# Row factors of a layer norm moved from the rows to the products, part of another norm moved to GpSimd, and a new order of all engines

## The chip, the cores and the metric

One core of a Trainium2 chip runs the whole program, and the metric is the time of one execution in device microseconds. Most executions of a kernel agree within 0.3%, so times are medians of several runs. A ratio is the mean time of one kernel's fast runs over that of the other's fast runs of the same rounds, with a 95% interval. It is therefore not quite the ratio of the medians quoted beside it. A profile is one more execution of the same program. Its span is about 1.7 us shorter than the reported time.

## The reference, cut to what matters

```python
def _layernorm(x, axis=-1, eps=1e-5): ...
xn = _layernorm(x)                              # x: 2048 x 640, the first layer norm
# branch A: attention, 32 heads of 20 channels
p = _softmax(q @ k.T * Dh ** -0.5)              # 32 x 2048 x 2048 exponentials
s = (p @ v) @ wo
# branch B
h = _gelu(_layernorm(xn) @ w1)                  # the second layer norm
hs = shifted_by_1_and_2_rows(h) @ w2
x1 = xn + hs
g = _silu(x1 + _gelu(_layernorm(x1) @ w3) @ w4)
out = x + s * g
```

The second layer norm acts on rows whose mean is already zero. All that is left of it is one factor for each row. Such a factor commutes with the product by w1.

## The kernel before

The program is a list of tasks. A planner in the kernel's own source books a duration for each of them, and a latency for each transfer. From these it makes one fixed order of instructions for every engine before anything runs.

```python
self.dma_bw = 280.0                              # bytes per ns
t.lat = self.dma_lat0 + nbytes / self.dma_bw     # dma_lat0 = 1900 ns, booked for every transfer
C_SP = 660                                       # ns of queue time booked for one transfer
# ... first layer norm, one task for each 128 rows ...
T("dve", c_dve(D, "4x"), lambda e, ...: e.tensor_scalar(dst_of(n), xn[:, n, :], mv[:, li, 0:1], rs[:, li:li + 1],
                                              op0=ALU.subtract, op1=ALU.mult), ...)
# ... and, for the rows whose statistics ScalarE made:
T("act", c_act(D) + 40, lambda e, ...: e.activation(xn[:, n, :], xn[:, n, :], AF.Identity, bias=sv[:, 7, ...], scale=sv[:, 6, ...]), ...)
# ... second layer norm and w1, for each chunk of 512 rows ...
T("dve", c_dve(KC * 516, "1x"), fy, ...)         # y2c = xnT * row factors, all of a chunk in one multiply
for m in range(KC):
    h, wa = self.mm_tile(f"w1_{ch}_{m}", ...)    # products of y2c and w1
    T("dve", c_dve(512), lambda e, ...: e.tensor_copy(hx[:, ch, m, :], self.wbank(h)[:, 0:512]), ...)
# ... softmax normalisation of one group of heads and one chunk of queries ...
T("dve", ..., lambda e: e.tensor_copy(Ob, PV bank), ...)
T("sp", ...: dz <- sums)   T("sp", ...: ZT <- dz)                  # spread the sums over the partitions
T("dve", c_dve(16, "recip"), lambda e: e.reciprocal(RZ, ZT), ...)
T("sp", ...: dr <- RZ)     T("sp", ...: RB <- dr, broadcast, 256 KB)   # store and load again
T("dve", c_dve(512, "1x"), lambda e: e.tensor_tensor(dst, Ob, RB, op=ALU.mult), ...)
```

(The cuts are marked by dots, and the last lines are shortened to what moves where.) Two engines share the exponentials. ScalarE takes most of them with its exponential function, and VectorE the rest through integer arithmetic. A table of blocks says how many go to VectorE.

## Time and profile before

| | before |
|---|---|
| time, median of 4 runs | 891.04 us (890.24 to 892.52) |
| span of the profiled run | 889.4 us |
| first exponential starts | 36.26 us |
| last exponential ends | 878.10 us |
| ScalarE idle in between | 16.2 us |

ScalarE is the bound, as the prediction shows. So the execution is cut in three at its first and its last exponential. The view of stretches below gives the length of each, then the busy time and instruction count of TensorE, its weight loads, VectorE, ScalarE and GpSimd, and last the granted TensorE clock (the share of full speed that TensorE was allowed), and the DMA's share and rate.

```profile
0.00:36.26 36.26, 23.83 (x670) 14.79 (x670) 27.24 (x92) 25.33 (x48) 23.77 (x47) 1.00 0.46 143
36.26:878.10 841.84, 802.08 (x14914) 348.30 (x14912) 689.27 (x896) 825.66 (x853) 14.07 (x22) 1.00 0.21 58
878.10:889.40 11.30, 3.34 (x56) 0.99 (x48) 7.84 (x14) 0.00 (x1) 0.00 (x0) 0.70 0.21 73
```

Three groups of VectorE's instructions in that kernel (busy us, mean ns of one, then the idle time just before them and what ended it):

```profile
L1479 DVE TENSOR_TENSOR arena<-arena 128x512 bf16<-128x512 f32 x28 | 19.3, 689 | 16.1 <-DMA arena<-recips 15.8
...
L1695 DVE CAST arena<-psum 128x512 bf16<-128x512 f32 x20 | 13.7, 687 | 2.3 <-PE psum L771 2.1
...
L1682 DVE TENSOR_TENSOR arena<-arena 128x2580 bf16<-128x2580 bf16 x2 | 5.7, 2838 | 0.0
```

The last two are the evictions of w1's products (each copies a product out of PSUM, the memory that TensorE writes) and half of the row scaling that the change removes. The first is the multiply by the broadcast reciprocals.

### The profile page before, as it was taken

The page shows a single profiled execution, that of the slowest core. Times are in us where ns is not written, and L with a number is a line of the kernel's source. Part 1 is how long each engine was busy: PE and PEld are TensorE (multiplying, and loading weights), DVE is VectorE, ACT ScalarE, POOL GpSimd, SP SyncE. Part 2 cuts the span into 40 slices and gives each one's busy share as a digit, 9 for nine tenths or more (in the row PEclk, how much of TensorE's full clock was granted, in tenths as well). Part 3 has the DMA queues.
Part 4 walks back from the last instruction along what each step waited for, and adds up shares of the span by engine and source line. Part 5 has one row for each costly group of instructions (what it writes and reads, how often), then busy time and mean ns, then how long its engine had stood idle before and what let it go on. Part 6 is the DMA issues. An engine that isn't in the chain of part 4 may idle for free.

```text
span 889.4 us, 34152 instructions
## 1 busy us (share of the span) xinstructions
PE 829.2 (93%) x15630; PEld 364.1 (41%) x15630; DVE 724.4 (81%) x1000; ACT 851.0 (96%) x900; POOL 37.8 (4%) x69
## 2 busy tenths in 40 slices
PE   4999999999999999999998999999999799998996
PEld 2434333334444433344443544433434344444453
DVE  7756888887888899989776779987878679797895
ACT  6899999999999999999998999999999999999994
POOL 7310000000000000000000000000000000010000
PEclk9999999999999999999999999999999999999998
DMA  6003300012210013222223031222222201114322
GB/s 222 11 14 87 94 22 25 25 43 77 80 48 29 22 46 86 62 61 57 62 53 98 20 95 35 72 84 59 54 60 51 82 10 53 47 53 126 105 63 76
DMA packets 83548, 54.81 MB, mean 62 GB/s; under 512 B 52556, under 2 KB 77340, under 8 KB 83276
## 3 DMA queue, kind: packets, MB, share of 16 engines
q1 hardware_dynamic: 83404, 52.62, 21.1%
q8 instruction: 123, 2.02, 0.9%
q14 instruction: 21, 0.17, 0.1%
HBM read 37.91 MB, written 10.63 MB: 55 GB/s over the span
## 4 chain that ended last, share of the span: by engine, by line
ACT 45%; PE 27%; DVE 19%; DMA 8%; issue 1%; SPq 0%
ACT arena L1404 42%; PE psum L771 11%; PE psum L1380 8%; DVE arena L1345 4%; DVE arena L1431 4%; DMA arena<-recips 4%; PE psum L1362 3%; PE psum L1319 3%; PE psum L1354 2%; DMA recips<-arena 2%; DVE arena L970 2%; DMA queries<-arena 1%; ACT arena L1756 1%; ACT arena L1698 1%; DVE arena L1682 1%
## 5 line engine op out<-in xcount | busy, mean ns | idle before, releaser
L1404 ACT ACTIVATE arena<-psum 128x1024 bf16<-128x1024 f32 x836 | 779.9, 1036 | 16.5 <-PE psum L1362 5.6
L1380 PE MATMUL psum<-arena 128*32 128x512 bf16 x4992 | 380.0, 381 | 11.5 <-ACT arena L1404 9.5
L771 PE MATMUL psum<-arena 128*32 128x320 bf16 (+1 forms) x5952 | 360.3, 335 | 7.8 <-DVE arena L1161 3.5
L1431 DVE TENSOR_SCALAR arena<-psum 128x1024 uint16<-128x1024 f32 x188 | 229.1, 1218 | 52.9 <-PE psum L1362 51.8
L1345 DVE TENSOR_SCALAR arena<-arena 128x4096 uint16<-128x4096 uint16 (+1 forms) x236 | 230.1, 1008 | 5.4 <-PE psum L1354 4.1
L771 PEld LDWEIGHTS psum<-arena 128*32 128x32 bf16 x5952 | 147.9, 97 | 148.0 <-issue 27.4
L1380 PEld LDWEIGHTS psum<-arena 128*32 128x32 bf16 x4992 | 106.8, 95 | 145.6 <-ACT arena L1404 102.6
L1319 PE MATMUL psum<-arena 128*22 128x512 bf16 x1672 | 161.6, 381 | 2.0 <-DVE arena L1466 1.7
L1354 PE MATMUL psum<-arena 128*22 128x512 bf16 x1504 | 123.3, 380 | 2.1 <-DVE arena L1345 1.9
L1362 PE MATMUL psum<-arena 32*128 32x512 bf16 x800 | 83.7, 386 | 14.3 <-ACT arena L1404 6.6
L1319 PEld LDWEIGHTS psum<-arena 128*22 128x22 bf16 x1672 | 42.4, 92 | 54.2 <-issue 7.5
L1362 PEld LDWEIGHTS psum<-arena 32*128 32x128 bf16 x800 | 21.4, 91 | 98.8 <-ACT arena L1404 81.7
L1354 PEld LDWEIGHTS psum<-arena 128*22 128x22 bf16 x1504 | 36.4, 92 | 45.5 <-DVE arena L1345 10.6
L1753 DVE CAST arena<-psum 128x512 bf16<-128x512 f32 x48 | 33.0, 687 | 14.1 <-PE psum L771 14.1
L1205 DVE CAST arena<-psum 128x512 bf16<-128x512 f32 x40 | 27.3, 685 | 18.1 <-PE psum L771 18.1
L1479 DVE TENSOR_TENSOR arena<-arena 128x512 bf16<-128x512 f32 x28 | 19.3, 689 | 16.1 <-DMA arena<-recips 15.8
L1550 DVE SCALAR_TENSOR_TENSOR arena<-psum,arena 128x320 bf16<-128x320 f32 x32 | 15.5, 487 | 15.4 <-PE psum L771 15.4
L970 DVE BATCH_NORM_STATS2 arena<-arena 128x6 f32<-128x320 bf16 x52 | 23.0, 482 | 2.8 <-DMA arena<-in_A_x_dram 2.8
L1466 DVE COPY arena<-psum 128x512 f32<-128x512 f32 x28 | 19.2, 687 | 3.6 <-PE psum L1354 2.8
L1767 DVE TENSOR_TENSOR arena<-psum,arena 128x320 bf16<-128x320 f32 x32 | 15.5, 485 | 6.8 <-PE psum L771 6.8
L1756 ACT ACTIVATE arena<-arena 128x12288 bf16<-128x12288 bf16 x2 | 20.9, 10444 | 0.0
L1069 PE MATMUL psum<-arena 128*32 128x128 bf16 x320 | 9.3, 246 | 12.2 <-DVE arena L984 11.8
(101 smaller groups left out, 281.2 us busy)
## 6 DMA issues: line engine op xcount, KB each, us to landing
arena<-in_B_w_dram SPq DMA_DIRECT2D x48, 160.0 KB, 2.6
arena<-recips SPq DMA_DIRECT2D x28, 256.0 KB
arena<-arena SPq DMA_DIRECT2D x124, 32.0 KB, 1.9
arena<-in_B_w_dram SPq DMA_DIRECT2D x4, 960.0 KB, 5.3
arena<-in_A_x_dram SPq DMA_DIRECT2D x8, 320.0 KB, 6.1
arena<-in_A_x_dram SPq DMA_DIRECT2D x16, 160.0 KB, 2.5
out_dram<-arena SPq DMA_DIRECT2D x16, 160.0 KB, 1.8
arena<-keys SPq DMA_DIRECT2D x28, 80.0 KB
```

The lines of the kernel that those rows point to most:

```text
L771: ins = e.matmul(pb[32 * c:32 * c + 32, 0:N], lhsT(k, c), rhs(k, c), start=(k == 0), stop=(stop and k == nk - 1), tile_position=(0, 32 * c))
L970: lambda e, li=li, n=n, hh=hh: e.bn_stats(st[:, li, 6 * hh:6 * hh + 6], xn[:, n, hD * hh:hD * hh + hD]),
L1205: T("dve", c_dve(512), lambda e, h=h, c=c: e.tensor_copy(KS[:, 512 * c:512 * c + 512], self.wbank(h)[:, 0:512]), reads=[wa], writes=[A("KS ...
L1319: ins = e.matmul(pb[32 * i:32 * i + 22, 0:512], VA[:, ql, kts[i // 2], i, :], PT[:, slots[i // 2][0].slot, 512 * (i % 2):512 * (i % 2) + 512],
L1345: T("dve", c_dve(w, "4x"), lambda e, v=v, dst=dst: e.tensor_scalar(dst, U[:, ub, 0:w], 0.5, EXP_B[v], op0=ALU.mult, op1=ALU.add), reads=ha ...
L1354: ins = e.matmul(pb[32 * i:32 * i + 22, 0:512], wv, dst[:, at:at + 512].bitcast(BF16), start=first, stop=final, tile_position=(0, 32 * i))
L1362: return e.matmul(out, self.KT[32 * i:32 * i + 32, b, 128 * kt:128 * kt + 128], self.QT[32 * i:32 * i + 32, b, 512 * qc:512 * qc + 512], s ...
L1380: ins = e.matmul(out[32 * c:32 * c + 32, :], self.KT[:, b, 128 * kt + 32 * c:128 * kt + 32 * c + 32], self.QM[:, gb, 2 * a + jj, :], start ...
L1404: lambda e: e.activation(self.PT[:, hp.slot, :], self.psum[:, 512 * hs.slot:512 * hs.slot + 1024], AF.Exp, scale=cfg.scale),
L1431: ins = e.tensor_scalar(U[:, ub, 1024 * at + 512 * k:1024 * at + 512 * k + w], self.psum[:, 512 * hd.slots[k]:512 * hd.slots[k] + w], a_ex ...
L1753: T("dve", c_dve(512), lambda e, h=h, fc=fc, i=i: e.tensor_copy(GT[:, i, fc, :], self.wbank(h)[:, 0:512]), reads=[wa], writes=at, name=f"g ...
L1756: T("act", 2750 + c_act(2 * FC * 512), lambda e: e.activation(GT[:, :, :, :], GT[:, :, :, :], AF.Gelu_apprx_tanh), reads=gta, writes=gta, ...
```

## The change

It has three parts, which the diff shows cut to its core: the row factors move into the evictions of w1's products, four of the sixteen first-norm tiles go to GpSimd, and the planner books transfers differently, with new due times, a new table of blocks and a few more planner settings that are not shown.

```diff
-        self.dma_bw = 280.0
+        self.dma_bw = 223.0
-            t.lat = self.dma_lat0 + nbytes / self.dma_bw
+            t.lat = self.dma_lat0 + nbytes / self.dma_bw + dlat      # dlat: -840 for the reciprocals' store, +1100 for their load ...
-C_SP = 660
+C_SP = 400
-        self.DUE = dict(k0=-37.9, k1=-9.1, ...)
+        self.DUE = dict(k0=100.3, k1=-164.3, ...)                    # all due times
-        self.ND = ([2, 2, 3, 3], ... [4, 2, 3, 2])                   # blocks of exponentials for VectorE: 94
+        self.ND = ([1, 2, 3, 3], ... [4, 3, 1, 2])                   # 95
+        self.POOLN = [1, 9, 13, 15]
...
-            T("dve", c_dve(D, "4x"),
+            pool = ve_out and n in cfg.POOLN
+            T("pool" if pool else "dve", 160 + 0.86 * D if pool else c_dve(D, "4x"),      # subtract, then multiply
...
+            if n in self.cfg.POOLN:
+                T("pool", 160 + 0.86 * D, ... op0=ALU.mult, op1=ALU.add) ...               # instead of ScalarE
...
-            T("dve", c_dve(KC * 516, "1x"), fy, ...)
             for m in range(KC):
+                T("sp", C_SP * len(ranges), fr, ...)                 # row factors of this tile, broadcast, 256 KB
...
-                T("dve", c_dve(512), ... e.tensor_copy(hx[:, ch, m, :], self.wbank(h)[:, 0:512]), ...)
+                T("dve", c_dve(512), ... e.tensor_tensor(hx[:, ch, m, :], self.wbank(h)[:, 0:512], RR[:, r, :], op=ALU.mult), ...)
```

## The prediction

> **What bounds the kernel now.** I read the page of the profile first: busy time by engine, then the 40 slices, then the chain that ended last.
>
> ```profile
> PE 829.2 (93%) x15630; PEld 364.1 (41%) x15630; DVE 724.4 (81%) x1000; ACT 851.0 (96%) x900; POOL 37.8 (4%) x69
> ...
> PE   4999999999999999999998999999999799998996
> PEld 2434333334444433344443544433434344444453
> DVE  7756888887888899989776779987878679797895
> ACT  6899999999999999999998999999999999999994
> ...
> ACT 45%; PE 27%; DVE 19%; DMA 8%; issue 1%; SPq 0%
> ```
>
> ScalarE (ACT) is the bound: 96% busy, a 9 in nearly every slice, and the largest share of the chain. Its idle time is 889.4 - 851.0 = 38.4 us. TensorE is a close second, so it decides whether ACT has something to read. The table of groups says what ACT does and for whom it waits:
>
> ```profile
> L1404 ACT ACTIVATE arena<-psum 128x1024 bf16<-128x1024 f32 x836 | 779.9, 1036 | 16.5 <-PE psum L1362 5.6
> ```
>
> That is 836 exponentials at 779.9/836 = 0.933 us each in a row (the 1036 ns of one overlap). The timeline of ACT alone shows where the 38.4 us lie:
>
> ```profile
> 36.26 75.28 ACT L1404 ACTIVATE arena<-psum 128x1024 bf16<-128x1024 f32 x81 [0.48 <-PE psum L1362]
> 112.32 30.85 ACT L1404 ACTIVATE arena<-psum 128x1024 bf16<-128x1024 f32 x33 [0.79 <-PE psum L1380]
> 143.75 1.02 ACT L1404 ACTIVATE arena<-psum 128x1024 bf16<-128x1024 f32 x1 [0.58 <-PE psum L1362]
> ...
> 656.31 1.02 ACT L1404 ACTIVATE arena<-psum 128x1024 bf16<-128x1024 f32 x1 [1.31 <-PE psum L1362]
> ```
>
> The first exponential starts at 36.3 us and the last ends at 878.1. Before it lies the head (layer norm, transposes, first projections) with 10.9 us of ACT idle; after it an 11.3 us tail; between them, 841.8 us of which ACT is busy 825.7 by the view of stretches, so 16.2 us idle, in about two dozen gaps of 0.2 to 1.6 us. So nothing but the count of ACT's work, the head, the tail and those gaps can move the time.
>
> What feeds the gaps is in the chain of waits in order of time (start, length, what):
>
> ```profile
> 125.69 0.60 DVE arena L1695
> 126.29 2.75 DVE arena L1682
> 129.04 1.14 DVE arena L1345
> 130.18 1.13 DVE arena L1431
> 131.32 0.17 DVE arena L1473
> 131.49 0.02 issue
> 131.50 3.08 DMA recips<-arena
> 134.59 5.06 DMA arena<-recips
> ```
>
> The 2.75 us is the old row scaling, one multiply of all of a 512-token chunk. The short reciprocal L1473 of the softmax sums stands behind it, then two transfers of 8.1 us, and this ends in ACT's gaps at 143 (0.58 and 0.17). The same picture stands at 175.9, ending at 193. Other gaps follow the same pair of transfers without a row scaling before it: 345 (0.82), 373 (0.44), 476 to 481 (2.5 in four gaps), 586 (0.44), 656 (1.5). Together 0.75 + 0.73 + 0.82 + 0.44 + 2.5 + 0.44 + 1.5 = 7.2 us of the 16.2 come out of this transfer chain.
>
> **What the Trainium skill says.** "VectorE: DVE Perf Modes", section "The perf-mode tier table": a tensor_tensor reading PSUM or fp32 runs at 1x, and so does a copy of fp32 from PSUM. The trace agrees, in two groups of the same size, one a multiply or add with a second operand and one a plain cast:
>
> ```profile
> L1767 DVE TENSOR_TENSOR arena<-psum,arena 128x320 bf16<-128x320 f32 x32 | 15.5, 485 | 6.8 <-PE psum L771 6.8
> ...
> L1266 DVE CAST arena<-psum 128x320 bf16<-128x320 f32 x32 | 15.4, 488 | 5.2 <-PE psum L771 4.3 <-PE psum L1069 0.7
> ```
>
> 485 against 488 ns: a multiply inside an eviction is free. "GPSIMD Engine Reference", section "Engine selection": one-input elementwise work is roughly line-rate there, two-input work some 2x slower. The trace has a one-input TENSOR_SCALAR on 128x176 in 340 ns where nothing disturbs it. "TensorEngine Tiling (Array Packing)", section "Key Properties": changing the tiling mode drains TensorE. The trace agrees: at 484.4 eight matmuls of 320 columns are followed by scores of the other shape after 0.38 us where eight such take 0.27 otherwise, some 0.1 us per change.
>
> **The change, part by part.**
>
> *Row factors.* Removed: four multiplies of 2826 to 2839 ns on VectorE, 11.3 us. Added: nothing in count, since the 20 casts of w1's products (687 ns) become multiplies by a row-factor tile; by the comparison above, still 687. The products use the unscaled transposed rows, whose factors commute with the matmul. The price is transfers: one 1 MB broadcast (5.1 us from issue to landing) becomes 20 of 256 KB in 32 issues, 5 MB. At the 1 MB in 5.1 us of the trace, about 200 GB/s, an estimate, that is 26 us of transfer, in the stretch between 90 and 240 us or so where the DMA share is 5 to 32%. Seven buffers run ahead. I take it as hidden. VectorE is not the bound, so its 11.3 us are worth only what they bring forward: the reciprocals at 131 and 181.
>
> *First layer norm.* Rows 1 and 9 leave VectorE (about 0.39 us each) and rows 13 and 15 leave ACT: 5.1 us for six, 0.85 each, so ACT loses 1.7 us in the head. On GpSimd one such of 640 elements is an estimate from the 340 ns for 176: 0.8 to 1.2 us. Rows 13 to 15 were three in series on ACT from 26.5 to 29.0, and the last transposes (30.15) waited for them; now one on ACT runs beside two on GpSimd. In the built order 140 instead of 220 matmuls of 320 columns stand ahead of the first scores. After the last transposes the old order has 88 + 4 matmuls of 512 columns (at 47 ns) and 28 of 320 (34 ns), 5.3 us; the new one 60 + 4 and 40, 4.4 us. I book 2.0 us for the head: 1.2 from the norms, 0.8 from the matmuls, a little under the 0.9 that they differ by.
>
> *Split of the exponentials.* The table of blocks goes from 94 to 95 and each moves two tiles from ACT to VectorE: 834 exponentials, -2 x 0.933 = -1.9 us of ACT. VectorE gets 188 tiles in one piece and two in halves: four halves of some 0.69, +2.8 us. Its wide steps change from 140 long and 96 short to 156 and 68: 16 x 1.196 - 28 x 0.652 = +0.9. VectorE in sum: -11.3 + 2.8 + 0.9 - 0.8 = -8.4 us. TensorE: 64 fewer column-shaped score matmuls (0.43 us per eight) is -3.5; 16 more row-shaped in four groups, 4 x 0.33 = +1.3; 12 more of the value products, +0.6; six more changes of shape there and back, 216 visits for 210, +1.2. In sum -0.4: nothing. TensorE stays as near to the bound as it was.
>
> *Order.* All engines are reordered. The old planner put the broadcast of reciprocals at 1900 ns + 256 KB at 280 GB/s = 2.8 us, where the trace has 5.06; the new one books 1900 + 1175 + 1100 = 4.2. It also books 400 instead of 660 ns of queue time per issue. So the steps that wait on this chain should be placed where their data has arrived. This, with the earlier reciprocals, is where the 7.2 us of gaps can come back. A new order makes new gaps of its own; I book 6.5 us net out of the 16.2. The tail is built as before: four transposes and multiplies after the last value product, then the four last output tiles; its last value products have 8 fewer fillers of 34 ns ahead, -0.3.
>
> Sum: -1.9 - 2.0 - 6.5 - 0.3 = -10.7 us of span, 889.4 to 878.7; the reported time was 1.7 above the span, so 880.4.
>
> **Rivals.** (a) The 20 broadcasts sit in the one in-order queue of SyncE and delay the reciprocal chain. The waits of that queue show 27.6 us in front of the second transfer already; in the new order up to eleven row-factor issues stand between the sums' first transfer and its second. For it: each such broadcast must wait for its buffer. Against it: a normalisation round has some 26 us and the chain needs about 11. Were it so, gaps of 1 to 2 us would come back in four or five rounds, and the time would be 884 to 888. (b) TensorE becomes the bound: its 93% hide shape changes and the clock (0.92 in the slices around 467 and 689). Then removing VectorE's and ACT's work gives nothing but the head: 886. Against it: between 36 and 878 us it is busy 802.1 of 841.8 us, so 39.7 idle against ACT's 16.2. (c) GpSimd's norms are slow or delay the row factors' powers behind them on that in-order engine: the head then gains nothing, 882. (d) The order is near perfect: all 16.2 us of gaps go instead of 6.5, 871.
>
> **Range and chances.** The certain part is 1.9 of ACT; the head is between 0 and 4, the gaps between +2 and -13. That makes 872.5 to 888 the range for 8 in 10. Faster by over 2% needs 873.3, all of the gaps and the head: 0.09. Slower by over 2% needs 18 us of new waits in an order planned with better numbers: 0.03.
>
> **What would show it.** ACT at 834 exponentials and about 847.5 us busy (-1.9, -1.7); VectorE near 716; w1's evictions as multiplies at about 687 ns; first exponential near 34.3; ACT idle between first and last exponential near 10 instead of 16.2; the tail near 11. I am wrong if the w1 multiplies are slower or wait for the row factors, if ACT's gaps lie behind the transfer of reciprocals as before, or if the gaps now come from TensorE with VectorE and DMA long done.

## The result, and the profile after

| | before | after | difference |
|---|---|---|---|
| time, median of 4 runs | 891.04 | 885.78 (884.17 to 886.2) | -5.3 |
| ratio | | 0.9936 [0.9918, 0.9954] | |
| span of the profiled run | 889.4 | 884.1 | -5.3 |
| head, to the first exponential | 36.26 | 35.65 | -0.6 |
| middle, ScalarE busy | 825.66 | 823.33 | -2.3 |
| middle, ScalarE idle | 16.2 | 14.1 | -2.1 |
| tail, after the last exponential | 11.30 | 11.04 | -0.3 |

The change is 0.6% faster, which is the "same" of the prediction, and the time lies inside the range, 5.4 us above the 880.4 of the prediction's sum. The differences sum to the 5.3 us. They come from the view of stretches after:

```profile
0.00:35.65 35.65, 20.01 (x592) 12.83 (x596) 28.07 (x86) 23.61 (x46) 30.37 (x50) 1.00 0.46 145
35.65:873.06 837.41, 800.30 (x14962) 348.22 (x14957) 680.52 (x889) 823.33 (x851) 12.55 (x24) 1.00 0.24 63
873.06:884.10 11.04, 2.53 (x52) 0.80 (x44) 7.61 (x13) 0.00 (x0) 0.00 (x0) 0.78 0.22 76
```

In the head, TensorE and ScalarE work less than before, yet the stretch is hardly shorter. GpSimd is the engine that grew, from 23.77 to 30.37 us. VectorE grew by 0.8 us although two norms had left it.

The page of the changed kernel, with the busy times, the chain that ended last and the exponentials' group:

```profile
PE 822.8 (93%) x15594; PEld 361.9 (41%) x15594; DVE 716.2 (81%) x986; ACT 846.9 (96%) x896; POOL 42.9 (5%) x74
...
ACT 55%; PE 19%; DVE 17%; DMA 5%; POOL 1%; issue 1%; POOLq 0%
...
L1444 ACT ACTIVATE arena<-psum 128x1024 bf16<-128x1024 f32 x834 | 777.8, 1038 | 14.4 <-PE psum L1420 5.0
```

ScalarE's share of the chain rose from 45% to 55%, and that of the DMA fell from 8% to 5%. That is the direction the change meant. Its groups that answer to those shown of before, and the two kinds of norm on GpSimd:

```profile
L1519 DVE TENSOR_TENSOR arena<-arena 128x512 bf16<-128x512 f32 x28 | 19.2, 686 | 11.5 <-DMA arena<-recips 11.4
...
L1734 DVE TENSOR_TENSOR arena<-psum,arena 128x512 bf16<-128x512 f32 x20 | 13.7, 687 | 8.7 <-PE psum L782 8.7
...
L999 POOL TENSOR_SCALAR arena<-arena 128x640 bf16<-128x640 bf16 x2 | 5.1, 2534 | 0.1
...
L1037 POOL TENSOR_SCALAR arena<-arena 128x640 bf16<-128x640 bf16 x2 | 1.7, 875 | 1.8 <-DVE arena L1032 1.8
```

The multiply in the eviction takes 687 ns as the cast did, so the row scaling is indeed free. The wait for the reciprocals fell from 15.8 to 11.4 us, but did not go. On GpSimd a norm written as multiply-then-add takes 875 ns, and one written as subtract-then-multiply 2534 ns.

The largest cluster of gaps in the changed kernel stands at 209 us. The chain of waits (start, length, what) leads to it:

```profile
197.41 0.17 DVE arena L1513
197.58 0.02 issue
197.60 4.04 DMA recips<-arena
201.64 0.02 issue
201.66 5.53 DMA arena<-recips
207.19 0.02 issue
207.21 0.04 DVE arena L1519
207.25 0.57 issue
207.82 1.23 DVE arena L1471
```

The pair of transfers took 9.6 us. VectorE stood 2.86 us before its multiply, TensorE 2.43 us behind VectorE, and ScalarE 2.18 us behind TensorE, as the three timelines show:

```profile
207.21 0.69 DVE L1519 TENSOR_TENSOR arena<-arena 128x512 bf16<-128x512 f32 x1 [2.86 <-DMA arena<-recips]
...
209.18 0.40 PE L1388 MATMUL psum<-arena 32*128 32x512 bf16 x4 [2.43 <-DVE arena L1471]
...
209.62 1.02 ACT L1444 ACTIVATE arena<-psum 128x1024 bf16<-128x1024 f32 x1 [2.18 <-PE psum L1388]
```

Then TensorE's matmuls ran slowly for 4 us. The first of the next two lines is eight score matmuls in that stretch, the second the same eight a little later:

```profile
210.16 1.01 PE L1420 MATMUL psum<-arena 128*32 128x512 bf16 x8
...
214.66 0.60 PE L1420 MATMUL psum<-arena 128*32 128x512 bf16 x8
```

The granted clock from 208 to 216 was 0.78 and 0.80 in windows of 4 us, and 1.00 on both sides. ScalarE's gaps of the whole cluster, 2.18 + 0.57 + 0.68 and five smaller ones of 0.17 to 0.28, sum to 4.5 us of the 14.1.

The planner's own bookings tell where the chip left the plan. It had booked the first exponential at 31.5 us, and it came at 35.65. The exponential at 138 us ran 4.3 us behind its booking, and the one at 245 us 8.9 behind. From there to the end the distance stayed between 8.4 and 10.7. So most of what the plan missed was lost in the head and around 209. The plan of the kernel before, read the same way, was 3.5 us short at the first exponential and 12.4 at the end of the last. The two plans end the last exponential at 865.7 and 863.6 us. By the planner's own numbers, each with its own bookings, the change thus promised 2.1 us there, and the chip gave 5.0. The 10.7 us of the prediction stood in neither plan.

### The profile page after: what moved, and what is told of

The parts are those of the page before. It is cut to its first block, busy times and chain, and to the rows that moved or that the text cites. A ratio compares the mean times of both kernels' runs of the same rounds, so it can differ in the third digit from the quotient of the medians.

```text
span 884.1 us, 34138 instructions
## 1 busy us (share of the span) xinstructions
PE 822.8 (93%) x15594; PEld 361.9 (41%) x15594; DVE 716.2 (81%) x986; ACT 846.9 (96%) x896; POOL 42.9 (5%) x74
## 4 chain that ended last, share of the span: by engine, by line
ACT 55%; PE 19%; DVE 17%; DMA 5%; POOL 1%; issue 1%; POOLq 0%
ACT arena L1444 53%; PE psum L782 8%; PE psum L1420 6%; DVE arena L1371 5%; DVE arena L1471 4%; DMA arena<-recips 3%; PE psum L1345 2%; PE psum L1388 2%; DMA recips<-arena 2%; PE psum L1380 1%; ACT arena L1809 1%; DVE arena L984 1%; ACT arena L1825 1%; DVE arena L1805 1%; DVE arena L1225 1%
## 5 line engine op out<-in xcount | busy, mean ns | idle before, releaser
L1420 PE MATMUL psum<-arena 128*32 128x512 bf16 x4928 | 375.7, 381 | 8.0 <-ACT arena L1444 6.6
L1471 DVE TENSOR_SCALAR arena<-psum 128x1024 uint16<-128x1024 f32 (+1 forms) x192 | 231.5, 1206 | 42.1 <-PE psum L1388 41.3
L1345 PE MATMUL psum<-arena 128*22 128x512 bf16 x1668 | 161.8, 381 | 1.2 <-DVE arena L1506 0.6
L1380 PE MATMUL psum<-arena 128*22 128x512 bf16 x1520 | 126.5, 380 | 2.5 <-DVE arena L1371 2.2
L1519 DVE TENSOR_TENSOR arena<-arena 128x512 bf16<-128x512 f32 x28 | 19.2, 686 | 11.5 <-DMA arena<-recips 11.4
L1286 DVE CAST arena<-psum 128x320 bf16<-128x320 f32 x32 | 15.4, 488 | 10.9 <-PE psum L782 10.5
L1089 PE MATMUL psum<-arena 128*32 128x128 bf16 x320 | 8.9, 248 | 13.7 <-DVE arena L999 13.1
```

The lines of the kernel that those rows point to most:

```text
L1345: ins = e.matmul(pb[32 * i:32 * i + 22, 0:512], VA[:, ql, kts[x // 2], i, :], PT[:, slots[x // 2][0].slot, 512 * (x % 2):512 * (x % 2) + 512],
L1380: ins = e.matmul(pb[32 * i:32 * i + 22, 0:512], wv, dst[:, at:at + 512].bitcast(BF16), start=first, stop=final, tile_position=(0, 32 * i))
L1420: ins = e.matmul(out[32 * c:32 * c + 32, :], self.KT[:, b, 128 * kt + 32 * c:128 * kt + 32 * c + 32], self.QM[:, gb, 2 * a + jj, :], start ...
L1471: ins = e.tensor_scalar(U[:, ub, 1024 * at + 512 * k:1024 * at + 512 * k + w], self.psum[:, 512 * hd.slots[k]:512 * hd.slots[k] + w], a_ex ...
```

## The experiments

Theory at the outset: the gain is smaller than predicted because of two places, the head, where GpSimd holds up others, and the gaps, where the order still stands on bookings that do not hold. The rivals: the row factors' broadcasts delay the reciprocals (rival a of the prediction), GpSimd's norms are slow (rival c), or TensorE's clock takes back what is won (part of rival b). Seven kernels are meant to tell them apart. All were run beside the kernel before.

| run | time, median | ratio to before |
|---|---|---|
| e1_memset_later | 886.36 | 0.9928 [0.991, 0.9945] |
| e2_rr_small | 886.52 | 0.9932 [0.9909, 0.9954] |
| e3_norm_form | 886.12 | 0.993 [0.9902, 0.9957] |
| e4_before_rows | 893.16 | 1.0011 [0.9983, 1.0039] |
| e5_after_nopool | 886.58 | 0.9939 [0.9912, 0.9966] |
| e6_busy | 885.5 | 0.9923 [0.9899, 0.9947] |
| e7_measured | 880.81 | 0.989 [0.9868, 0.9911] |

### e1_memset_later: a clear on GpSimd moved by 1 us

In the head of the changed kernel, a VectorE instruction on four elements per partition took 2.15 us. TensorE's next four matmuls, ScalarE's next step and the first exponential waited for it. VectorE's timeline, then GpSimd's:

```profile
31.72 2.15 DVE L1166 TENSOR_SCALAR arena<-arena 128x4 bf16<-128x4 f32 x1
```

```profile
31.69 2.15 POOL L951 MEMSET arena<- 128x2048 bf16 x1
```

The two cover each other to within 0.03 us at the start. The experiment keeps everything and lets the clear wait for the small instruction:

```diff
-        T("pool", 1500, lambda e: e.memset(self.QT[:, 1, :], 0.0), writes=[A("QT0")], name="qt0")
+        T("pool", 1500, lambda e: e.memset(self.QT[:, 1, :], 0.0), reads=[A("Mq")], writes=[A("QT0")], name="qt0")
```

> The changed kernel, same order on every engine; only the clearing of one 2048-wide buffer on GpSimd now waits until the tiny VectorE scaling L1166 (128x4) has been done. Theory A (the head lost its gain because that VectorE instruction cannot start while GpSimd clears the buffer: 2155 ns instead of 237): the scaling takes some 0.24 us, the first exponential comes 1.5 to 1.9 us earlier (33.8 to 34.1 instead of 35.65), and the time falls by as much, to about 884. Rival (the scaling is slow for another reason, or the head is bound by the transposes): it still takes 2 us, or the first exponential moves less than 0.4 us; time 885.8.

Measured: the small instruction took 0.29 us, and TensorE's wait for it went.

```profile
32.57 0.29 DVE L1166 TENSOR_SCALAR arena<-arena 128x4 bf16<-128x4 f32 x1
```

In all three kernels where the clear lies over it (after, e2, e3) the instruction took 2.13 to 2.16 us. In the ten other profiled runs it took 0.24 to 0.38. That is shown. What it is worth in time is not resolved: the ratio is 0.9928 against 0.9936. The first exponential came at 34.63 us in this run, and in two repeats below at 33.79 and 34.94, so one execution's head moves by over 1 us by itself (the first load of x landed between 3.62 and 4.10 us in the traces). Here the first exponential came 1.0 us earlier and not the 1.5 to 1.9 expected. The small instruction started 0.85 us later than in the kernel after, and before it 20 matmuls at 18.70 us had taken 1.55 us in place of 1.04. And the profiled run gave its lead back at 497 us, in a gap of 4.26 us where the kernel after has 0.71. The lines of TensorE there, in the kernel after and in this one:

```profile
490.61 0.74 PE L1053 MATMUL psum<-arena 128*32 128x128 bf16 x32 [1.91 <-DVE arena L1063]
492.50 4.64 PE L782 MATMUL psum<-arena 128*32 128x512 bf16 x84 [1.16 <-DVE arena L1181]
```

```profile
486.45 0.74 PE L1053 MATMUL psum<-arena 128*32 128x128 bf16 x32 [1.91 <-DVE arena L1063]
488.98 7.57 PE L782 MATMUL psum<-arena 128*32 128x512 bf16 x84 [1.79 <-DVE arena L999]
```

It is the same order of the same instructions, but the 84 products take 7.57 instead of 4.64 us, at a granted clock of 0.52 and 0.63 in the two windows from 488 to 496. The edit alone does not decide it: e2 does not have it and ran them in 4.65, while e3 does not have it either, ran at 0.61 and 0.54 there and took 7.53:

```profile
491.29 4.65 PE L782 MATMUL psum<-arena 128*32 128x512 bf16 x84 [1.47 <-DVE arena L1519]
```

```profile
489.82 7.53 PE L782 MATMUL psum<-arena 128*32 128x512 bf16 x84 [1.61 <-DVE arena L999]
```

It need not be mere chance either. Of the looks at this order without other work for TensorE, four had their first exponential before 35 us (e1, e3, and e8 and e10 below). In all four TensorE waited 1.51 to 1.79 us just before the 84 products, and these were slow. In the three whose first exponential came at 35.65 or later (after, e2, e5) it waited 1.00 to 1.47 us and they were fast. So a shorter head may itself lengthen this wait and lose its lead here. Seven looks suggest that and do not show it.

### e2_rr_small: the row factors' broadcasts made small

```diff
+                w = 512 if KC * ch + m < 7 else 16
-   ... e.dma_start(RR[f0:f1, r, :], ... [1, 512])
+   ... e.dma_start(RR[f0:f1, r, 0:w], ... [1, w])
```

The result is wrong, since only 16 columns of most tiles are fresh, although its error stayed under the threshold of the comparison.

> The changed kernel, same order; the row-factor loads after the first seven move 16 columns instead of 512 (wrong result on purpose). Theory B (the cluster of gaps of ACT between 209 and 224 us, 4.5 us, comes from a row-factor load issued 1.3 us ahead of the reciprocals' transfer on the same queue): the transfer of reciprocals at 197.6 lands in about 2.3 instead of 4.04 us, VectorE's wait for the reciprocals' broadcast (2.86 us) shrinks to about 1, and the cluster to 1 to 2.5 us; time 883 to 884. Rival (the order itself puts the multiply by the reciprocals too early, whatever the loads do): the cluster stays above 4 us and the time at 885.8.

Measured: at 199 us the store of the reciprocals took 2.74 us from its issue to the next instead of 4.04, VectorE's wait before the multiply fell from 2.86 to 1.20, and all such waits from 11.4 to 9.9 us. ScalarE's gaps of the cluster at 209 fell from 4.5 to 1.5 us, the first of them from 2.18 to 0.52. So the local part came out nearly as expected, and the broadcasts do lengthen this chain, as rival (a) says. But the time did not move (0.9932; 883 to 884 us were expected). ScalarE's idle time in the whole middle stretch was 13.7 us against 14.1, so other gaps grew instead. Of the 1.5 us by which VectorE's waits fell, 1.1 stand before 250 us, where the broadcasts run.

### e3_norm_form: the cheap form of the norm for rows 1 and 9

```diff
-   op0=ALU.subtract, op1=ALU.mult
+   op0=ALU.mult if pool else ALU.subtract, op1=ALU.add if pool else ALU.mult
```

The result is wrong: the operands stay the mean and the factor.

> The changed kernel, same order; the two GpSimd normalisations of rows 1 and 9 do multiply-then-add instead of subtract-then-multiply (wrong result on purpose). Theory C (the 2.53 us of each is the form of the operation: the other two, multiply-then-add on the same size, took 0.875): 0.85 to 0.9 us each. Rival (it is contention with VectorE at that moment): still above 2 us. For the time: if GpSimd at 9 to 12 us is on the head's path the first exponential comes up to 1 us earlier; if the 2.2 us wait at L1166 sets the head, less than 0.3.

```profile
L999 POOL TENSOR_SCALAR arena<-arena 128x640 bf16<-128x640 bf16 x2 | 1.8, 875 | 0.1
```

The two norms took 875 ns instead of 2534. The operations alone make this difference, since operands, shapes and types are the same. TensorE's second group of transposes started at 13.87 us, against 14.60 in the kernel after. The first exponential came at 34.70, though the 2.14 us of the clear was still there. The time is 0.993. So rival (c) is right about the mechanism, at 0.7 us of the head, and too small for the times to show.

### e4_before_rows: the old order with the row factors alone

```diff
-    Gen(nc, aps, cfg).build()
+    ref = Gen(*scratch(aps), Cfg(..., old=True, rows=False, pool=False))     # the kernel before, only planned
+    ref.build(plan_only=True)
+    cfg = Cfg(..., old=True, rows=True, pool=False)
+    cfg.KEEP = ref.pl             # TensorE, ScalarE and VectorE keep the order of before
+    Gen(nc, aps, cfg).build()
```

> The kernel before with its own order kept on TensorE, ScalarE and VectorE; only the row factors are moved to w1's products (four multiplies of 2.83 us gone, 20 casts become multiplies, 1 MB load becomes 32 loads of 5 MB together). Theory D (the row factors alone are worth at most the gaps that follow the old scaling, 1.5 us): 889 to 891. Rival 1 (worth nothing, or less than nothing because of the loads): 891 to 894. Rival 2 (they carry the whole gain of the change): 886 to 887.

Measured: 1.0011. Taking 11.3 us from VectorE is worth nothing that the times resolve by itself, as the first rival of this run expected. In the profile VectorE's waits for the reciprocals rose from 15.8 us in 12 places to 20.9 in 17:

```profile
L1595 DVE TENSOR_TENSOR arena<-arena 128x512 bf16<-128x512 f32 x28 | 19.3, 689 | 21.1 <-DMA arena<-recips 20.9
```

One of them, of 3.40 us at 109.6, was followed by a wait of 2.35 for TensorE behind VectorE and a gap of 2.67 for ScalarE behind TensorE, with a granted clock of 0.82 and 0.76 in the 8 us after it. The kernel before waited 0.94 us at that place. So rival (a) happens in the old order. But the broadcasts are issued between 91 and 170 us, and up to 250 us the waits rose only from 4.8 to 6.3. The other 3.6 us of the rise stand later, where no broadcast runs, and stay unexplained. One reservation: the edit keeps the order of TensorE, ScalarE and VectorE, but the queue of transfers and GpSimd were planned again. The queue differs in 17 places, all before 200 us of the plan.

### e5_after_nopool: the new order without GpSimd's norms

The edit is as in e4, with the kernel after as the one whose order is kept, the row factors in and the norms back on VectorE and ScalarE.

> The changed kernel's order on every engine, but the four first-norm tiles 1, 9, 13 and 15 go back to where they were (two to VectorE at about 0.4 us each, two to ScalarE at about 0.9 us each); the row factors stay. Theory: the GpSimd part is worth next to nothing, because two of its four norms run as subtract-then-multiply at 2.53 us and hold TensorE's first transposes as long as they help; then 885 to 887 us (ratio to before 0.992 to 0.996) with the first exponential between 35.2 and 36.5 us. Rival: the GpSimd part carried most of the gain, then 888 to 891 us (ratio 0.997 to 1.0) with the first exponential after 37 us. With the run in which row factors alone gave 1.001 this leaves the order as the rest.

Measured: 0.9939, against 0.9936 for the whole change. The time is that of the theory, but the first exponential came at 37.49, where only the rival had expected it (after 37). That is 1.8 us later than after. As in e4, the transfers were planned again, against what the expectation says: the second and the third load of x changed places, and VectorE waited 0.77 us for the one that now came later. The middle was 0.95 us shorter. So the 1.8 us are not GpSimd's norms alone. If the 0.77 are taken off, the norms buy some 1 us of the head, an estimate, and nothing that the times resolve. The difference between e5 and e4, 0.9939 against 1.0011, is 0.7% or some 6 us: it is the new order with its block table and bookings, and these two intervals do not overlap. It is all of the gain that the times resolve. The new order without the row factors was not run, so whether it needs them is open.

### e6_busy: TensorE kept busy where its clock fell

Based on e1, TensorE multiplies the identity by itself into a bank that nobody reads, while it waits before the 84 products, and before 80 others that had taken 4.51 us in the kernel after and 6.18 in e1. The edit, shortened here, also moves one group of transposes behind two groups of value products.

```diff
+                if ename == "pe" and t.name in BUSY:
+                    for p in t.before: eng.wait_ge(sems[tasks[p].eng], tasks[p].seq)     # the bank's last reader
+                    self.busy(eng, t.tile_handle, BUSY[t.name])                           # 16, 12 and 24 groups of four small products, 128 columns each
```

> The kernel with the late clear, and TensorE given products that nobody reads while it waits at two places where the earlier run showed its clock fall to half: before the transposes' end and before the 84 products near 489 us, and before the 80 products near 689 us. Theory (the clock follows TensorE's own idling): the 84 products take 4.6 to 5.0 us instead of 7.57, the 80 take 4.5 instead of 6.18, the ScalarE gap near 497 us falls from 4.26 to 0.7 to 1.5 us, no window from 484 to 496 has a granted clock below 0.9, and the time is 882.5 to 884.5 us (ratio 0.989 to 0.9915). Rival (the clock falls whatever TensorE does, or the gap comes from the wait itself): the products still take over 6 us, the gap stays over 3 us, and the time stays at 885.5 to 887 us.

Measured: the 84 products took 4.64 us and the 80 took 4.51, as the theory wants, and the clock stayed at 1.00 from 484 to 496. But the time is 0.9923, not to be told from e1's 0.9928. As the kernel after had run both groups fast without any help, this was one look at something that varies. So both kernels were looked at twice more, one run each, whose state is unknown:

> The kernel with the late clear once more, for one more look at where its granted clock falls: so far it fell at both of the last two gelu stages in that kernel, at neither, or at one in others of the same order. If TensorE's idling there is what lets it fall, and chance decides which windows, a repeat shows the 84 products at 4.6 or at 7.6 us and the 80 at 4.5 or 6.2, at least one of them slow.

> The kernel with the idle products once more. If keeping TensorE busy is what kept its clock up, the 84 products take 4.6 to 4.7 us and the 80 take 4.5 again; if the first look was chance, one of them is slow here (over 6 us).

> As the repeat of the kernel with the late clear before it: at least one of the two groups of products slow (over 6 us) if TensorE's idling lets the clock fall there.

> As the repeat of the kernel with the idle products before it: both groups of products fast (under 4.8 us) if being busy is what keeps the clock up.

| | the 84 products, us | the 80 products, us | time of that look, us |
|---|---|---|---|
| e1, e8, e10 (late clear) | 7.57, 6.71, 5.90 | 6.18, 4.51, 4.51 | (e1: median 886.36), 885.15, 885.79 |
| e6, e9, e11 (and busy) | 4.64, 4.64, 6.33 | 4.51, 4.51, 4.51 | (e6: median 885.5), 884.09, 887.2 |

The 5.90 of e10 already misses its expectation (over 6) by a little. The last run of e6's kernel is the clear miss:

```profile
489.70 6.33 PE L821 MATMUL psum<-arena 128*32 128x512 bf16 x84 [0.44 <-DVE arena L1559]
```

TensorE had been busy for 3.01 of the 4 us before 488, and the clock still fell to 0.72. So work of this kind does not keep the clock up for certain, and whether it helps at all is open: six looks do not settle it. What is shown is that a fall costs 1.3 to 2.9 us of products and up to 3.5 us of ScalarE's gap, and that it comes and goes between executions of one kernel. The kernel before has such falls as well (below).

### e7_measured: bookings taken from the traces, and the order searched on them

If wrong bookings are behind the gaps that are left, an order made on measured times should take them away. This kernel has the late clear. It leaves the cheap norms of rows 13 and 15 on GpSimd and gives the dear ones of rows 1 and 9 back to VectorE. Its order was searched anew by single moves in the planner, with these bookings changed: GpSimd's norm from 0.71 to 2.53 us, VectorE's norm from 0.23 to 0.36, the reciprocals' store 1 us and their load 0.5 us longer, GpSimd's clears as measured. In the traces that store had taken 1.4 to 4.0 us to the issue that waited for it, where the plan of the change books some 1.5.

```diff
+MOVES = {'pe': [(127, 122), ...],      # 344 tasks of TensorE, each with the task that it now follows
+         'dve': [...], 'pool': [...], 'sp': [...]}      # 215, 32 and 110; ScalarE's order is unchanged
+    cfg.POOLN = [13, 15]
```

> The kernel with the late clear; GpSimd's two subtract-then-multiply norms go to VectorE (the two multiply-then-add ones stay); and the order of TensorE, VectorE and the transfers searched again by single moves, with the plan's bookings replaced by what the traces showed (GpSimd norm 2.53 us, VectorE norm 0.36 us, reciprocals' store 1 us and load 0.5 us longer than booked, GpSimd clears 1.25 to 3.5 us). ScalarE's own order is unchanged. In that plan the first exponential comes 1.8 us earlier than with the late clear alone, the gaps fall from 14.0 to 6.5 us, and the last exponential ends 10.6 us earlier. Theory (the gaps that the change left are mostly wrong bookings and order, so an order made on measured times takes them away): first exponential 32.5 to 34.5 us, gaps 7 to 10 us, time 876 to 881 us (ratio 0.983 to 0.988). Rival (what is left is TensorE's clock and the chance of transfers, which no order reaches): gaps stay at 12 to 14 us and the time at 884 to 886.5 us (ratio over 0.991).

Measured: 880.81 us, ratio 0.989 [0.9868, 0.9911], the fastest of all, 10.7 us under the kernel before of its rounds and 5 us under the change.

```profile
0.00:34.18 34.18, 20.46 (x588) 13.22 (x592) 23.77 (x84) 23.73 (x46) 16.88 (x41) 1.00 0.31 98
34.18:867.92 833.74, 806.54 (x14966) 344.24 (x14962) 682.99 (x906) 822.35 (x851) 21.73 (x31) 1.00 0.24 66
867.92:879.00 11.08, 2.55 (x52) 0.82 (x44) 7.63 (x13) 0.00 (x1) 0.00 (x0) 0.78 0.22 75
```

```profile
L1560 DVE TENSOR_TENSOR arena<-arena 128x512 bf16<-128x512 f32 x28 | 19.2, 684 | 4.0 <-DMA arena<-recips 4.0
```

Against before, the head is 2.1 us shorter. ScalarE's idle time in the middle is 833.74 - 822.35 = 11.4 us instead of 16.2. VectorE waits 4.0 us for the reciprocals in place of 15.8, in 3 places in place of 12. The gap at 209 is gone. The theory holds in direction and nearly in size. The time is in its range, and the ratio just outside (0.983 to 0.988). The gaps that the timeline lists before the exponentials sum to 9.6 us where it expected 7 to 10 (12.6 in the kernel after), but the whole idle time of 11.4 us lies between theory and rival. About 2.5 us of what is left stand between 47 and 53 us, where a wait of 1.2 us was followed by a clock of 0.57. Three things were changed at once here, so the share of each is not told apart. A rival is that the renewed search found the gain and not the bookings. A search on the old bookings was not run. But this kernel's source still holds the change's bookings, and planned with these its order ends at 879.3 us, 2.1 us later than the change's at 877.2. So by the change's bookings this order is the worse one, and the chip runs it 5 us faster, which speaks for the new bookings.

## Why the prediction was right or wrong

The time was inside the range and the class was right. By its own steps:

- **ScalarE's work, -1.9: right.** 834 exponentials, and 2.3 us less busy time in the middle. The total, 846.9, was foretold as 847.5.
- **Row factors free in the evictions: right.** 687 ns as foretold. VectorE's sum is 716.2 against 716 foretold, in part by luck: 1.9 us of it are the small instruction that GpSimd's clear held. "I take it as hidden" was nearly right of the transfers: they cost some 1.1 us of VectorE's waits in the new order (e2) and 1.5 in the old one, where the time did not fall (e4).
- **The head, "I book 2.0 us": wrong in size, 0.6.** The step that failed is the term "1.2 from the norms". It took the cost of GpSimd from a multiply of 176 elements and did not ask which operations a norm has. Two of the four norms took 2.53 us, three times the form that had been looked at (e3: worth 0.7 us at the transposes). And a clear on GpSimd, newly placed by the order, held a small VectorE step on the way to the first exponential for 2.15 us (e1). With both mended, and another order, e7's head is 2.1 us shorter than before. Rival (c), "slow or delay", named the engine.
- **The gaps, "6.5 us net out of the 16.2": wrong in size, 2.1.** The failed term is that the new bookings place the steps "where their data has arrived". The new booking of the load, 4.2 us, was better than the old 2.8, but the load took 4.6 us and more. The store was booked shorter than before, at about 1.5 us against up to 4.0 measured. So the waits for this chain fell only from 15.8 to 11.4 us, and none of that before 250 us (4.8 to 5.5), where the prediction had hoped for the reciprocals at 131 and 181. The gaps that the prediction had pinned to it came back at other places, above all at 209, where a wait and the slow clock after it made 4.5 us of them. With measured bookings and a new search (e7) the waits fell to 4.0 us, and the idle time was 4.8 us less than before.
- **The tail, -0.3: right**, 11.04 against 11.30.
- **Rivals.** (a) is real and small where the broadcasts run: 1.1 us of VectorE's waits in the new order (e2), 1.5 in the old (e4). That alone does not explain why e4 gained nothing. (b): the clock's falls cost microseconds in single executions, but they were in the kernel before as well (0.57 at 476 us, 0.64 at 704), and how much of the difference they explain is open. (d) did not come.

So a gain of the size of -10.7 was there: e7's span is 879.0 against the 878.7 of the sum. That the two meet is in part luck, since e7 comes there with -4.8 in the gaps and -3.3 in ScalarE's work where the sum has -6.5 and -1.9. The change itself reached half of it.

## What to carry to other kernels

When a planned order decides the waits, first check its bookings against the trace, by the operation and its form and with the spread of each transfer. A better order was worth more here than 11 us of work taken from an engine that was not the bound. A helper engine is not free because it is idle: look for instructions on its neighbour that last as long as the helper's. And where one gap is followed by slow matmuls, take two or three looks before a cause is named, since that part changes from one execution to the next.

## What the Trainium skill lacked or had wrong

- "GPSIMD Engine Reference", section "Engine selection", calls one-input elementwise work roughly line-rate on GpSimd. Here the pair of operations decides: multiply-then-add with two per-partition operands took 875 ns on 128x640 bf16, subtract-then-multiply 2534 ns, against some 0.4 us on VectorE.
- "TensorE: Matmul & The Clock Gate", section "Why this matters for your kernels", wants no idle gaps above about 3 us between bursts of matmuls. The traces show half clock after less: after a wait of 2.43 us (after, at 209: groups of eight matmuls then followed each other in 0.85 us in place of 0.43), and after a longest wait of 1.2 us in a stretch where TensorE was busy for 2.80 of 4 us (e7, clock 0.57 from 48 to 52). The page's remark, in its section "What's actually happening", that the point of change varies from run to run agrees: the same 84 products took 4.64 to 7.57 us.
